# Sorted block attention with a two-layer network: instruction borders, order of loads and slots of work moved

## The chip, the cores and the metric

The kernel runs on one core of one Trainium2 chip. The metric is the device time of one execution in microseconds (us), as the median of several runs. A profile was taken of one execution; its times count from the start of its span. TensorE (PE in the profile, PEld for its weight loads) multiplies matrices, VectorE (DVE), ScalarE (ACT) and GpSimd (POOL) work on elements, SyncE (SP) issues transfers, and so does POOL here.

## The reference, cut to what matters

Four batches of eight heads, 768 tokens in eight blocks of 96, head size 64. A small 8x8 matrix for each head is normalized five times along its rows and columns (the Sinkhorn steps). It mixes the blocks of keys and values, and each block of queries attends to its mixed block. A two-layer network with a squared ReLU follows.

```python
P = sort_net                                  # (4, 8, 8, 8)
for _ in range(5):
    P = P - np.max(P, axis=-1, keepdims=True)
    P = np.exp(P)
    P = P / (np.sum(P, axis=-1, keepdims=True) + 1e-09)
    P = P / (np.sum(P, axis=-2, keepdims=True) + 1e-09)
k_sorted = np.einsum('bhij,bhjcd->bhicd', P, k_b)      # v_sorted likewise
scores = scale * np.matmul(q_b, k_sb.transpose(0, 1, 2, 4, 3))
attn = softmax(scores)
x = (attn @ v_sb)  # to (3072 tokens, 512)
h = x @ w_in                                  # 512 x 2048
g = s * np.maximum(h, 0) ** 2 + b
out = g @ w_out                               # 2048 x 512
```

Since out = s * (r*r) @ w_out + b * (column sums of w_out), the kernel adds b as a bias made of those column sums.

## The kernel before

The tokens are cut into eight tiles of 384, two for each batch. For each tile, `ffn1` is the first layer (64 products of 128x128 by 384 columns, eight pairs of PSUM banks) and `ffn2` the second (three blocks of 128 tokens, 16 products of 512 columns each). The attention of batch b+1 is laid between the products of batch b's second layer, by "slots": a table that names which piece is issued after which product. Batch 0's attention has nothing to hide behind, but its second half lies in the first layer of tile 0.

POOL issues the loads of k, q, v and of both weights, which come as float32 and land as bfloat16. PSUM has two pools here: `psa`, three buffers of two banks, and `psb`, two buffers of one bank.

The start, cut:

```python
    psa = ctx.enter_context(tc.tile_pool(name="psa", bufs=3, space=bass.MemoryType.PSUM))
    psb = ctx.enter_context(tc.tile_pool(name="psb", bufs=2, space=bass.MemoryType.PSUM))
# ...
    QTOK = {}

    def load_q(b):

        ti = rawp.tile([BLK, NB, H, D], BF, tag="rawq", name="qtok")
        qv = q[b].rearrange("h (n t) d -> t n h d", n=NB)
        for n in range(NB):
            nc.gpsimd.dma_start(out=ti[:, n], in_=qv[:, n])
        QTOK[b] = ti
# ...
    load("k", 0, 3)
    load_q(0)
    ones = const.tile([128, 32], BF)
    wi = const.tile([128, NHP, d_ff], BF)
    wo = const.tile([128, NF, d_model], BF)

    def load_w():
        wiv = moe_w_in.rearrange("(a p) f -> p a f", p=128)
        for c in range(2):
            cs = slice(c * (d_ff // 2), (c + 1) * (d_ff // 2))
            for a in range(NHP):
                nc.gpsimd.dma_start(out=wi[:, a, cs], in_=wiv[:, a, cs])
        fill_vs(0)
        wov = moe_w_out.rearrange("(f p) n -> p f n", p=128)
        for c in range(4):
            fs = slice(c * (NF // 4), (c + 1) * (NF // 4))
            nc.gpsimd.dma_start(out=wo[:, fs, :], in_=wov[:, fs, :])
# ...
    def warm(n, w=512):
        for _ in range(n):
            if not Z:
                Z.append(psb.tile([128, 512], FP, tag="b", name="z"))
            nc.tensor.matmul(out=Z[0][:, 0:w], lhsT=zeros[:, 0:128], rhs=zeros[:, 0:w],
                             start=True, stop=True)
# ...
    warm(60, 64)
    warm(30)
    for it in range(5):
        nc.scalar.activation(out=sn, in_=sn, func=AF.Exp)
        if it == 1:
            for d0 in range(0, D, D // 4):
                permute(nc.gpsimd, 0, v0f, slice(3 * CV, C2), slice(d0, d0 + D // 4))
        if 1 <= it <= 3:
            permute(nc.scalar, 0, v0f, slice((it - 1) * CV, it * CV))
        if it in (1, 2):
            idle[it - 1]()
        # ... sums, reciprocals and products of sn on DVE
```

`warm` keeps TensorE busy with products of zeros while DVE and ACT normalize `sn`. Each product of the kernel is two instructions, a weight load and a matmul. The normalized matrices are then spread over the partitions (`pe`), and turned into the moving matrices `pd` that mix keys and values:

```python
    def spread_p():

        PE_.append(psb.tile([128, B, NB, NB], FP, tag="b", name="pe"))
        for b in range(B):
            nc.tensor.matmul(out=PE_[0][:, b].rearrange("p i j -> p (i j)"), lhsT=emat[:, b, :],
                             rhs=sn.rearrange("p i j -> p (i j)"), start=True, stop=True)

    def take_p(b0, n):

        bs = slice(b0, b0 + n)
        tmp = rtp.tile([128, n * NB, NB], FP, tag=f"tmp{n}", name="tmp")
        nc.vector.tensor_tensor(out=tmp, in0=PE_[0][:, bs].rearrange("p b i j -> p (b i) j"),
                                in1=spread(jsel, [[0, n * NB], list(jsel.ap[1])]), op=ALU.mult)
        nc.vector.tensor_reduce(out=PT[:, bs].rearrange("p b i -> p (b i)"), in_=tmp, axis=AX.X,
                                op=ALU.add)
        cs = rtp.tile([128, n], FP, tag=f"cs{n}", name="cs")
        nc.vector.tensor_reduce(out=cs, in_=PT[:, bs], axis=AX.X, op=ALU.add)
        nc.vector.reciprocal(out=RC[:, bs], in_=cs)

    def build_pd(b):
        pd = const.tile([128, 2, 2, NG], BF, name=f"pd{b}")
        nc.vector.scalar_tensor_tensor(
            out=pd.rearrange("p e z (a i) -> p (e z a) i", i=NB),
            in0=spread(bm, [list(bm.ap[1]), [0, NB]]), scalar=RC[:, b:b + 1],
            in1=spread(PT[:, b], [[0, 4 * NHP], list(PT.ap[2])]), op0=ALU.mult, op1=ALU.mult)
        PD[b] = pd
```

Keys, values, scores, attention times values, and the transposes that make `xt` are pieces, of which `k_piece` shows the pattern; all but the transposes take a buffer of `psa`. Batches 1 to 3 have x transposed by a DMA (`t_dma`), and their queries likewise (`q_dma`).

```python
    def k_piece(b, c0, eng):
        src, mov, dst = RAW["k", b], PD[b], KS[b % 2]
        ps = psa.tile([128, CK, 2, NG], FP, tag="a", name="tp")
        for c in range(CK):
            for e in range(2):
                nc.tensor.matmul(out=ps[e * 64:(e + 1) * 64, c].rearrange("p z g -> p (z g)"),
                                 lhsT=src[:, c0 + c, :],
                                 rhs=mov[:, e].rearrange("p z g -> p (z g)"),
                                 start=True, stop=True)
        evac(eng, dst[:, :, :, c0:c0 + CK], ps.rearrange("p c z g -> p g z c"))
# ...
    def ffn1(t, slots, ahead=0):

        gt = gtp.tile([128, NF, TG], BF, tag="gt", name="gt")
        GT[t] = gt
        xt = XT.pop(t)
        H1 = {}

        def part(i, hpl):
            if i not in H1:
                H1[i] = psa.tile([128, 2, 512], FP, tag="a", name="hps")
            for f in range(2):
                for hp in hpl:
                    fc = (2 * i + f) * 128
                    nc.tensor.matmul(out=H1[i][:, f, 0:TG], lhsT=wi[:, hp, fc:fc + 128],
                                     rhs=xt[:, :, hp, :],
                                     start=(hp == 0), stop=(hp == NHP - 1))

        for i in range(ahead):
            part(i, (0, 1))
        for i in range(NF // 2):
            part(i, (2, 3) if i < ahead else range(NHP))
            rt = rtp.tile([128, 2, TG], BF, tag="rt", name="rt")
            h = H1.pop(i)[:, :, 0:TG]
            nc.scalar.activation(out=rt, in_=h, func=AF.Relu)
            nc.vector.tensor_tensor(out=gt[:, 2 * i:2 * i + 2, :], in0=rt, in1=rt, op=ALU.mult)
            for p in slots.get(i, ()):
                p()
```

`ffn2` runs its slots after every fourth product: slot m*4 + f//4. The order of the program after the Sinkhorn steps:

```python
    spread_p()
    take_p(0, 1)
    build_pd(0)
    warm(3)
    k_piece(0, 0, "A")
    k_piece(0, CK, "D")
    k_piece(0, 2 * CK, "A")

    nc.gpsimd.tensor_copy(out=ones[:, 0:1], in_=KS[0][:, 0, 0, 2 * CK:2 * CK + 1])
    load_w()
    q_piece(0, 0, "D")
    v_piece(0, 0, "A")
    v_piece(0, CK, "D")
    v_piece(0, 2 * CK, "A")
    v_piece(0, 3 * CK, "D")
    s_piece(0, 0, 0)
    s_piece(0, 0, 1)
    s_piece(0, 0, 2)
    warm(1)
    p_piece(0, 0, 0)
    s_piece(0, 0, 3)
    take_p(1, B - 1)
    warm(1)
    p_piece(0, 0, 1)
    warm(1)
    p_piece(0, 0, 2)
    Z.clear()
    t_piece(0, 0, 0, "A")
    p_piece(0, 0, 3)
    warm(3)
    t_piece(0, 0, 2, "D")
# ...
    def loads(b):
        load("k", b)
        load("v", b)
        load_q(b)
        v_sort(b)

    loads(1)
# ...
    def make_bias():
        cps = psa.tile([128, d_model], FP, tag="a", name="cps")
        for f in range(NF):
            r = slice(f % 4 * 32, f % 4 * 32 + 32)
            nc.tensor.matmul(out=cps[r], lhsT=ones, rhs=wo[:, f, :],
                             start=(f < 4), stop=(f >= NF - 4), tile_position=(0, f % 4 * 32))
        nc.vector.tensor_scalar(out=bias[0:32], in0=cps[0:32], scalar1=b_bc[0:32], scalar2=None,
                                op0=ALU.mult)
        for r in range(32, 128, 32):
            nc.vector.scalar_tensor_tensor(out=bias[0:32], in0=cps[r:r + 32], scalar=b_bc[r:r + 32],
                                           in1=bias[0:32], op0=ALU.mult, op1=ALU.add)
        for r in range(32, 128, 32):
            nc.scalar.copy(out=bias[r:r + 32], in_=bias[0:32])
# ...
    ffn1(0, {0: [QP(0, 1, "D")], 1: [SB(0, 1, 0)], 2: [SB(0, 1, 1)], 3: [P(0, 1, 0), SB(0, 1, 2)],
             4: [P(0, 1, 1), SB(0, 1, 3)], 5: [P(0, 1, 2)], 6: [P(0, 1, 3), TP(0, 1, 0, "A")],
             7: [TP(0, 1, 2, "D")]}, ahead=3)
    ffn1(1, {1: [PDB(1)], 3: [PDB(2)], 5: [PDB(3)], 6: [make_bias]}, ahead=3)
    for b in range(B):
        n = b + 1
        if b:
            if n < B:
                loads(n)
            ffn1(2 * b, {})
            ffn1(2 * b + 1, {})
        if n == B:
            ffn2(2 * b, {})
            ffn2(2 * b + 1, {})
            break
        q_dma(n)
        ffn2(2 * b, {0: [K(n, 0, "D"), K(n, 1, "A"), K(n, 2, "D")],
                     4: [V(n, 0, "D"), V(n, 1, "A"), V(n, 2, "D")],
                     8: [V(n, 3, "D"), SC(n, 0, 0), SC(n, 0, 1)],
                     11: [P(n, 0, 0), SC(n, 0, 2), SC(n, 0, 3)]})
        # ... the next tile's slots: the rest of the attention, t_dma after x
```

Of the kernel before, what the change touches and what calls it, by code (L numbers as in the profile page):

```python
# [22 lines left out]
def kernel(  # L23
# [66 lines left out]

    QTOK = {}

    def load_q(b):

        ti = rawp.tile([BLK, NB, H, D], BF, tag="rawq", name="qtok")
        qv = q[b].rearrange("h (n t) d -> t n h d", n=NB)
        for n in range(NB):
            nc.gpsimd.dma_start(out=ti[:, n], in_=qv[:, n])  # L98
        QTOK[b] = ti

    zeros = const.tile([128, 512], BF)
    nc.vector.memset(zeros, 0.0)  # L102
# [14 lines left out]
    nc.gpsimd.affine_select(out=emat, in_=emat, pattern=[[-H, B], [-1, H], [0, 2 * NB]], base=0,  # L117
                            channel_multiplier=1, compare_op=ALU.not_equal, fill=1.0)
    load("k", 0, 3)
    load_q(0)  # L120
    ones = const.tile([128, 32], BF)
    wi = const.tile([128, NHP, d_ff], BF)
    wo = const.tile([128, NF, d_model], BF)
# [1 line left out]
# [3 lines that stand above are left out]
            cs = slice(c * (d_ff // 2), (c + 1) * (d_ff // 2))  # L128
            for a in range(NHP):
                nc.gpsimd.dma_start(out=wi[:, a, cs], in_=wiv[:, a, cs])  # L130
        fill_vs(0)
        wov = moe_w_out.rearrange("(f p) n -> p f n", p=128)
        for c in range(4):
            fs = slice(c * (NF // 4), (c + 1) * (NF // 4))
            nc.gpsimd.dma_start(out=wo[:, fs, :], in_=wov[:, fs, :])
# [16 lines left out]
    def permute(eng, b, src, cs=slice(0, C2), ds=slice(0, D)):  # L152
# [4 lines left out]
        else:  # L157
# [14 lines left out]
    nc.vector.tensor_reduce(out=rstat, in_=sn, axis=AX.X, op=ALU.max)  # L172
    nc.vector.tensor_tensor(out=sn, in0=sn, in1=rstat.broadcast_to([BH, NB, NB]),
                            op=ALU.subtract)
    warm(60, 64)
    warm(30)
    for it in range(5):
        nc.scalar.activation(out=sn, in_=sn, func=AF.Exp)
        if it == 1:
            for d0 in range(0, D, D // 4):  # L180
                permute(nc.gpsimd, 0, v0f, slice(3 * CV, C2), slice(d0, d0 + D // 4))
        if 1 <= it <= 3:
            permute(nc.scalar, 0, v0f, slice((it - 1) * CV, it * CV))
        if it in (1, 2):
            idle[it - 1]()
        nc.vector.tensor_reduce(out=rstat, in_=sn, axis=AX.X, op=ALU.add)
        nc.vector.reciprocal(out=rrec, in_=rstat)
        nc.vector.tensor_tensor(out=sn, in0=sn, in1=rrec.broadcast_to([BH, NB, NB]), op=ALU.mult)
        if it == 4:
            break  # L190
        nc.vector.tensor_reduce(out=rstat, in_=sn.rearrange("p i j -> p j i"),
                                axis=AX.X, op=ALU.add)
        if it == 0:
            nc.vector.tensor_tensor(out=rstat, in0=rstat, in1=eps, op=ALU.add)
        nc.vector.reciprocal(out=rrec, in_=rstat)
        nc.vector.tensor_tensor(out=sn, in0=sn, in1=spread(rrec, [[0, NB], list(rrec.ap[1])]),
                                op=ALU.mult)
# [1 line left out]
    PD = {}  # L199
    PT = const.tile([128, B, NB], FP)  # L200
    RC = const.tile([128, B], FP)
    PE_ = []

    def spread_p():

        PE_.append(psb.tile([128, B, NB, NB], FP, tag="b", name="pe"))
        for b in range(B):
            nc.tensor.matmul(out=PE_[0][:, b].rearrange("p i j -> p (i j)"), lhsT=emat[:, b, :],
                             rhs=sn.rearrange("p i j -> p (i j)"), start=True, stop=True)

    def take_p(b0, n):

        bs = slice(b0, b0 + n)
        tmp = rtp.tile([128, n * NB, NB], FP, tag=f"tmp{n}", name="tmp")
        nc.vector.tensor_tensor(out=tmp, in0=PE_[0][:, bs].rearrange("p b i j -> p (b i) j"),
                                in1=spread(jsel, [[0, n * NB], list(jsel.ap[1])]), op=ALU.mult)
        nc.vector.tensor_reduce(out=PT[:, bs].rearrange("p b i -> p (b i)"), in_=tmp, axis=AX.X,
                                op=ALU.add)
# [5 lines that stand above are left out]
# [3 lines left out]
            in0=spread(bm, [list(bm.ap[1]), [0, NB]]), scalar=RC[:, b:b + 1],  # L227
            in1=spread(PT[:, b], [[0, 4 * NHP], list(PT.ap[2])]), op0=ALU.mult, op1=ALU.mult)
        PD[b] = pd

    def first_pd():
        spread_p()
        take_p(0, 1)
        build_pd(0)

    def evac(eng, out, in_):
        if eng == "A":
# [133 lines left out]
    def ffn1(t, slots, ahead=0):  # L371

        gt = gtp.tile([128, NF, TG], BF, tag="gt", name="gt")
        GT[t] = gt
        xt = XT.pop(t)
        H1 = {}

        def part(i, hpl):
# [8 lines that stand above are left out]

        for i in range(ahead):
            part(i, (0, 1))
        for i in range(NF // 2):  # L390
            part(i, (2, 3) if i < ahead else range(NHP))
            rt = rtp.tile([128, 2, TG], BF, tag="rt", name="rt")
# [5 lines that stand above are left out]
# [31 lines left out]
        nc.sync.dma_start(out=out[r0:r0 + 128, ns], in_=ot[:, ns])  # L429


    spread_p()
    take_p(0, 1)
    build_pd(0)
    warm(3)
    k_piece(0, 0, "A")
    k_piece(0, CK, "D")
# [12 lines left out]
    warm(1)  # L450
    p_piece(0, 0, 0)
    s_piece(0, 0, 3)
    take_p(1, B - 1)
    warm(1)
    p_piece(0, 0, 1)
    warm(1)
# [32 lines left out]
    def make_bias():  # L489
# [7 lines left out]
        for r in range(32, 128, 32):  # L497
            nc.vector.scalar_tensor_tensor(out=bias[0:32], in0=cps[r:r + 32], scalar=b_bc[r:r + 32],  # L498
                                           in1=bias[0:32], op0=ALU.mult, op1=ALU.add)
        for r in range(32, 128, 32):  # L500
            nc.scalar.copy(out=bias[r:r + 32], in_=bias[0:32])  # L501

# [8 lines left out]
    def QP(b, h, eng): return lambda: q_piece(b, h, eng)  # L511


    ffn1(0, {0: [QP(0, 1, "D")], 1: [SB(0, 1, 0)], 2: [SB(0, 1, 1)], 3: [P(0, 1, 0), SB(0, 1, 2)],
             4: [P(0, 1, 1), SB(0, 1, 3)], 5: [P(0, 1, 2)], 6: [P(0, 1, 3), TP(0, 1, 0, "A")],
             7: [TP(0, 1, 2, "D")]}, ahead=3)
    ffn1(1, {1: [PDB(1)], 3: [PDB(2)], 5: [PDB(3)], 6: [make_bias]}, ahead=3)
    for b in range(B):
        n = b + 1
        if b:  # L520
            if n < B:
                loads(n)
            ffn1(2 * b, {})
            ffn1(2 * b + 1, {})
        if n == B:
            ffn2(2 * b, {})
            ffn2(2 * b + 1, {})
            break
        q_dma(n)
        ffn2(2 * b, {0: [K(n, 0, "D"), K(n, 1, "A"), K(n, 2, "D")],  # L530
                     4: [V(n, 0, "D"), V(n, 1, "A"), V(n, 2, "D")],
                     8: [V(n, 3, "D"), SC(n, 0, 0), SC(n, 0, 1)],
                     11: [P(n, 0, 0), SC(n, 0, 2), SC(n, 0, 3)]})
        ffn2(2 * b + 1, {0: [P(n, 0, 1)], 1: [P(n, 0, 2)],
                         2: [P(n, 0, 3), TD(n, 0), SC(n, 1, 0), SC(n, 1, 1)],
                         4: [P(n, 1, 0)], 5: [P(n, 1, 1), SC(n, 1, 2), SC(n, 1, 3)],
# [31 lines left out]
```

The softmax here doesn't subtract the row's maximum and nothing guards it: scores larger than these inputs give would overflow.

## Time and profile before

The kernel takes 243.22 us (median of three runs, 243.13 to 243.81). The profiled execution has a span of 241.1 us.

| stage | from, us | to, us |
|---|---|---|
| warm-up of TensorE beside the Sinkhorn steps | 1.2 | 11.3 |
| `pe`, `pd`, keys, queries, values, scores of batch 0 | 11.3 | 29.6 |
| first layer of tiles 0 and 1 | 29.6 | 58.1 |
| column sums, bias, first keys of batch 1 | 55.6 | 65.5 |
| second layer of tiles 0 and 1, attention of batch 1 | 58.1 | 95.8 |
| first layer of tiles 2 and 3 | 95.8 | 116.8 |
| second layer of tiles 2 and 3, attention of batch 2 | 116.8 | 146.0 |
| the same for tiles 4 and 5 | 146.0 | 196.0 |
| tiles 6 and 7 | 196.0 | 241.1 |

| group | mean ns of one | count |
|---|---|---|
| hps, first layer, 384 columns | 326 | 512 |
| ops, second layer, 512 columns | 387 | 345 recorded |
| rt, ACT, 768 elements | 811 | 64 |
| gt, DVE, 768 elements | 597 | 64 |
| v moved by POOL (vp) | 884 | 24 |

Matmuls overlap, so a mean of 326 ns isn't what one adds: 128 of hps in a row take 20.80 us, 163 ns each. How to read the views: in the page, 40 slices show each engine's busy share in tenths, and PEclk the clock that TensorE was granted. A wait names the instruction that waited and what released it; "issue" means that the engine waited for nothing that the profile shows. The chain is the work that ended last, followed back from the end.

### The profile page before, as it was taken

Reading aid. Unit: us, or ns where it says so; the run is one execution under the profiler, and the core shown is the slowest. Engines: PE = TensorE matmul, PEld = TensorE weight load, DVE = VectorE, ACT = ScalarE, POOL = GpSimd, SP = SyncE. Lnnn points to the kernel's source line nnn. Section 1 sums busy time; section 2 is a strip of 40 time slices with the busy share of each in tenths; the row PEclk is TensorE's granted clock in tenths of the full one; section 3 lists DMA queues with packets and bytes.
Section 4 is the critical chain, followed back from the end, with each engine's and each line's share of the span. In section 5 each row is a group of like instructions: output and inputs, shape, how many; then the busy total and the mean of one; then the engine's idle time right before and its main releaser. Section 6 shows DMA issues by size and latency. Waiting matters only on the chain.

```text
span 241.1 us, 5694 instructions
## 1 busy us (share of the span) xinstructions
PE 221.9 (92%) x2481; PEld 133.0 (55%) x2507; DVE 122.6 (51%) x227; ACT 96.1 (40%) x124; POOL 65.3 (27%) x101
## 2 busy tenths in 40 slices
PE   7975979998499997999999999999999999999994
PEld 6464646664355653666655555666656556654453
DVE  6654735659536554434654763444656544442221
ACT  4635338562503350565512423565223416651000
POOL 8577742539919927400000000000000000000000
PEclk9998699999779999999999999999999999999999
DMA  6999999999799699990011189300111450001112
GB/s 199 207 121 143 204 206 199 205 133 141 131 184 170 110 200 178 189 154 0 3 46 46 54 145 174 69 0 0 49 43 46 109 155 0 0 4 45 60 71 87
DMA packets 52777, 25.80 MB, mean 107 GB/s; under 512 B 44816, under 2 KB 47120, under 8 KB 52752
## 3 DMA queue, kind: packets, MB, share of 16 engines
q0 software_dynamic: 29712, 12.85, 43.7%
q1 hardware_dynamic: 23040, 12.59, 22.8%
q8 instruction: 19, 0.31, 0.5%
q14 instruction: 6, 0.05, 0.1%
HBM read 27.27 MB, written 6.29 MB: 139 GB/s over the span
## 4 chain that ended last, share of the span: by engine, by line
PE 82%; DVE 6%; DMA 4%; issue 4%; ACT 3%
PE hps L384 32%; PE ops L405 30%; PE z L148 4%; DMA xt<-x 4%; PE tv L286 3%; PE pv L336 3%; PE sc L301 3%; PE tp L249 2%; ACT rt L394 2%; PE ops L418 1%; DVE gt L395 1%; DVE x L342 1%; DVE bias L498 1%; PE tq L268 1%; ACT bias L501 1%
## 5 line engine op out<-in xcount | busy, mean ns | idle before, releaser
L384 PE MATMUL hps<-xt,wi 128*128 128x384 bf16 x512 | 85.4, 326 | 1.7 <-DMA xt<-x 1.6
L405 PE MATMUL ops<-wo,gt 128*128 128x512 bf16 x345 | 83.5, 387 | 2.4 <-issue 1.6
L394 ACT ACTIVATE rt<-hps 128x768 bf16<-128x768 f32 x64 | 51.7, 811 | 53.2 <-PE hps L384 53.2
L384 PEld LDWEIGHTS <-wi 128*128 128x128 bf16 x512 | 49.3, 98 | 35.0 <-DMA xt<-x 2.1
L395 DVE TENSOR_TENSOR gt<-rt 128x768 bf16<-128x768 bf16 x64 | 38.2, 597 | 52.4 <-ACT rt L394 49.8
L405 PEld LDWEIGHTS <-gt 128*128 128x128 bf16 x368 | 34.3, 100 | 38.2 <-issue 3.0
L426 DVE SCALAR_TENSOR_TENSOR ot<-ops,s_bc,bias 128x512 f32<-128x512 f32 (+1 forms) x25 | 18.2, 730 | 41.1 <-PE ops L405 38.9
L306 ACT ACTIVATE at<-sc 112x768 bf16<-112x768 f32 x28 | 21.2, 807 | 34.3 <-PE sc L301 34.1
L98 POOL DMA_DIRECT2D qtok<-in_q_dram x32 | 24.7, 783 | 29.1 <-DMA rawk<-in_k_dram 10.4
L342 DVE TENSOR_TENSOR x<-pv,rec 96x512 bf16<-96x512 f32 x32 | 22.0, 687 | 1.1
L158 POOL COPY vp<-rawv 128x384 bf16<-128x384 bf16 x24 | 20.1, 884 | 0.0
L336 PEld LDWEIGHTS <-at 112*128 112x128 bf16 (+1 forms) x256 | 14.2, 106 | 7.0 <-issue 0.8
L240 DVE CAST vs<-tv 112x1024 bf16<-112x1024 f32 x11 | 13.2, 1222 | 5.6 <-PE tv L286 5.5
L336 PE MATMUL pv<-vs,at 112*128 112x66 bf16 (+1 forms) x256 | 14.8, 202 | 0.3 <-issue 0.3
L148 PE MATMUL z<-zeros 128*128 128x64 bf16 (+1 forms) x96 | 12.7, 301 | 1.6 <-DVE zeros L102 1.2
L238 ACT CAST vs<-tv 112x1024 bf16<-112x1024 f32 x5 | 5.1, 1018 | 17.1 <-PE tv L286 17.1
L249 PE MATMUL tp<-pd,rawk 128*64 128x64 bf16 x384 | 7.6, 200 | 4.4 <-ACT rt L394 2.0
L286 PEld LDWEIGHTS <-vp 128*64 128x64 bf16 x512 | 8.8, 113 | 3.6 <-issue 3.1
L286 PE MATMUL tv<-pd,vp 128*64 128x64 bf16 x512 | 9.8, 197 | 0.8 <-issue 0.7
L249 PEld LDWEIGHTS <-rawk 128*64 128x64 bf16 x384 | 7.0, 116 | 6.3 <-issue 6.3
L341 DVE RECIPROCAL rec<-pv 96x8 f32<-96x8 f32 x32 | 6.4, 199 | 7.9 <-PE pv L336 7.9
L301 PE MATMUL sc<-qt,ks 64*128 64x96 bf16 x224 | 7.9, 211 | 2.5 <-issue 2.5
(68 smaller groups left out, 100.6 us busy)
## 6 DMA issues: line engine op xcount, KB each, us to landing
out_dram<-ot SPq DMA_DIRECT2D x23, 256.0 KB, 2.5
qtok<-in_q_dram POOLq DMA_DIRECT2D x32, 96.0 KB, 10.9
rawk<-in_k_dram POOLq DMA_DIRECT2D x3, 768.0 KB, 7.7
rawv<-in_v_dram POOLq DMA_DIRECT2D x3, 768.0 KB, 12.0
wi<-in_moe_w_in_dram POOLq DMA_DIRECT2D x8, 256.0 KB, 8.5
wo<-in_moe_w_out_dram POOLq DMA_DIRECT2D x4, 512.0 KB, 13.6
v0f<-in_v_dram SPq DMA_DIRECT2D x4, 384.0 KB, 4.3
rawk<-in_k_dram POOLq DMA_DIRECT2D x3, 256.0 KB, 8.1
```

Of the source, the lines that this page charges most:

```text
L98: nc.gpsimd.dma_start(out=ti[:, n], in_=qv[:, n])
L148: nc.tensor.matmul(out=Z[0][:, 0:w], lhsT=zeros[:, 0:128], rhs=zeros[:, 0:w], start=True, stop=True)
L158: eng.tensor_copy(out=o, in_=i)
L249: nc.tensor.matmul(out=ps[e * 64:(e + 1) * 64, c].rearrange("p z g -> p (z g)"), lhsT=src[:, c0 + c, :], rhs=mov[:, e].rearrange("p z g -> ...
L286: nc.tensor.matmul(out=ps[z * GAP:(z + 1) * GAP, d, :], lhsT=VP[b % 2][:, d0 + d, :], rhs=PD[b][:, :, z, :], start=True, stop=True)
L306: nc.scalar.activation(out=at, in_=sc[0:KR, :, 0:TG], func=AF.Exp, scale=scale)
L336: nc.tensor.matmul(out=pv[0:m, e, n * VW:(n + 1) * VW], lhsT=atf[:, c0:c0 + m], rhs=VS[b % 2][:, e * NG + g0 + n, :], start=True, stop=True)
L342: nc.vector.tensor_tensor(out=x[:, :, hp * 128:(hp + 1) * 128].rearrange("p n (e d) -> p e n d", e=2), in0=pvv[:, :, :, 0:D], in1=rec.unsq ...
L384: nc.tensor.matmul(out=H1[i][:, f, 0:TG], lhsT=wi[:, hp, fc:fc + 128], rhs=xt[:, :, hp, :], start=(hp == 0), stop=(hp == NHP - 1))
L394: nc.scalar.activation(out=rt, in_=h, func=AF.Relu)
L395: nc.vector.tensor_tensor(out=gt[:, 2 * i:2 * i + 2, :], in0=rt, in1=rt, op=ALU.mult)
L405: nc.tensor.matmul(out=ops, lhsT=gt[:, f, m * 128:(m + 1) * 128], rhs=wo[:, f, :], start=(f == 0), stop=(f == NF - 1))
```

## The change

It has five parts. (1) The warm-up has 66 products more, small ones, so that the borders of the instruction blocks[...] fall elsewhere. (2) `pe` is made for batch 0 alone first; the others' part is copied from PSUM to SBUF by ACT, and used later, in the first layer of tile 1. (3) The last quarter of batch 0's v is moved by ACT and not by POOL, and the second half of q comes behind the first half of w_in, so that w_in can be issued once the keys are moved. (4) The slots of tile 0's first layer are shifted, the last transpose goes into tile 1, the column sums go to the end of tile 1's first layer, the bias's copies and the next batch's keys to later slots of the second layer. (5) The loads of batches 2 and 3 wait, by a one-element copy on POOL, for the first result of a first layer.

```diff
-    def load_q(b):
-        ti = rawp.tile([BLK, NB, H, D], BF, tag="rawq", name="qtok")
+    def load_q(b, ns=range(NB)):
+        if b not in QTOK:
+            QTOK[b] = rawp.tile([BLK, NB, H, D], BF, tag="rawq", name="qtok")
         qv = q[b].rearrange("h (n t) d -> t n h d", n=NB)
-        for n in range(NB):
-            nc.gpsimd.dma_start(out=ti[:, n], in_=qv[:, n])
-        QTOK[b] = ti
+        for n in ns:
+            nc.gpsimd.dma_start(out=QTOK[b][:, n], in_=qv[:, n])
# ...
     load("k", 0, 3)
-    load_q(0)
+    load_q(0, range(HB))
     ones = const.tile([128, 32], BF)
# ...
                 nc.gpsimd.dma_start(out=wi[:, a, cs], in_=wiv[:, a, cs])
+            if c == 0:
+                load_q(0, range(HB, NB))
         fill_vs(0)
# ...
                             op=ALU.subtract)
-    warm(60, 64)
-    warm(30)
+    warm(140, 64)
+    warm(16)
     for it in range(5):
         nc.scalar.activation(out=sn, in_=sn, func=AF.Exp)
-        if it == 1:
-            for d0 in range(0, D, D // 4):
-                permute(nc.gpsimd, 0, v0f, slice(3 * CV, C2), slice(d0, d0 + D // 4))
-        if 1 <= it <= 3:
+        if it >= 1:
             permute(nc.scalar, 0, v0f, slice((it - 1) * CV, it * CV))
# ...
     RC = const.tile([128, B], FP)
-    PE_ = []
-    def spread_p():
-        PE_.append(psb.tile([128, B, NB, NB], FP, tag="b", name="pe"))
-        for b in range(B):
-            nc.tensor.matmul(out=PE_[0][:, b].rearrange("p i j -> p (i j)"), lhsT=emat[:, b, :],
+    PB = const.tile([128, B - 1, NB, NB], FP)
+    def spread_p(b0, n):
+        pe = psa.tile([128, n, NB, NB], FP, tag="a", name="pe")
+        for b in range(n):
+            nc.tensor.matmul(out=pe[:, b].rearrange("p i j -> p (i j)"), lhsT=emat[:, b0 + b, :],
                              rhs=sn.rearrange("p i j -> p (i j)"), start=True, stop=True)
-    def take_p(b0, n):
+        return pe
+    def take_p(b0, n, pe):
# ...
         tmp = rtp.tile([128, n * NB, NB], FP, tag=f"tmp{n}", name="tmp")
-        nc.vector.tensor_tensor(out=tmp, in0=PE_[0][:, bs].rearrange("p b i j -> p (b i) j"),
+        nc.vector.tensor_tensor(out=tmp, in0=pe.rearrange("p b i j -> p (b i) j"),
                                 in1=spread(jsel, [[0, n * NB], list(jsel.ap[1])]), op=ALU.mult)
# ...
-    def first_pd():
-        spread_p()
-        take_p(0, 1)
-        build_pd(0)
# ...
         GT[t] = gt
-        xt = XT.pop(t)
+        xt = XT[t]
         H1 = {}
# ...
             part(i, (0, 1))
+        for p in slots.get(-1, ()):
+            p()
         for i in range(NF // 2):
# ...
-    spread_p()
-    take_p(0, 1)
+    take_p(0, 1, spread_p(0, 1))
     build_pd(0)
+    pe = spread_p(1, B - 1)
+    nc.scalar.copy(out=PB, in_=pe)
     warm(3)
# ...
     s_piece(0, 0, 3)
-    take_p(1, B - 1)
     warm(1)
# ...
+    def copy_bias():
         for r in range(32, 128, 32):
# ...
-    ffn1(0, {0: [QP(0, 1, "D")], 1: [SB(0, 1, 0)], 2: [SB(0, 1, 1)], 3: [P(0, 1, 0), SB(0, 1, 2)],
-             4: [P(0, 1, 1), SB(0, 1, 3)], 5: [P(0, 1, 2)], 6: [P(0, 1, 3), TP(0, 1, 0, "A")],
-             7: [TP(0, 1, 2, "D")]}, ahead=3)
-    ffn1(1, {1: [PDB(1)], 3: [PDB(2)], 5: [PDB(3)], 6: [make_bias]}, ahead=3)
+    ffn1(0, {2: [QP(0, 1, "D")], 3: [SB(0, 1, 0)], 4: [SB(0, 1, 1), P(0, 1, 0)],
+             5: [SB(0, 1, 2), P(0, 1, 1)], 6: [SB(0, 1, 3), P(0, 1, 2)],
+             7: [P(0, 1, 3), TP(0, 1, 0, "A")]}, ahead=3)
+    ffn1(1, {-1: [TP(0, 1, 2, "D")], 1: [lambda: take_p(1, B - 1, PB), PDB(1)], 4: [PDB(2)],
+             5: [PDB(3)], 7: [make_bias]}, ahead=3)
+    gate = const.tile([128, 1], BF)
+    def gated_loads(b):
+        def f():
+            nc.gpsimd.tensor_copy(out=gate, in_=GT[2 * b - 2][:, 0, 0:1])
+            loads(b)
+        return f
# ...
         if b:
-            if n < B:
-                loads(n)
-            ffn1(2 * b, {})
+            ffn1(2 * b, {0: [gated_loads(n)]} if n < B else {})
             ffn1(2 * b + 1, {})
# ...
         q_dma(n)
-        ffn2(2 * b, {0: [K(n, 0, "D"), K(n, 1, "A"), K(n, 2, "D")],
-                     4: [V(n, 0, "D"), V(n, 1, "A"), V(n, 2, "D")],
-                     8: [V(n, 3, "D"), SC(n, 0, 0), SC(n, 0, 1)],
-                     11: [P(n, 0, 0), SC(n, 0, 2), SC(n, 0, 3)]})
+        s0 = {1: [copy_bias]} if b == 0 else {}
+        s0.update({
+            2: [K(n, 0, "A"), K(n, 1, "D"), K(n, 2, "A")],
+            5: [V(n, 0, "D"), V(n, 1, "A"), V(n, 2, "D")],
+            9: [V(n, 3, "D"), SC(n, 0, 0), SC(n, 0, 1)],
+            11: [P(n, 0, 0), SC(n, 0, 2), SC(n, 0, 3)]})
+        ffn2(2 * b, s0)
         ffn2(2 * b + 1, {0: [P(n, 0, 1)], 1: [P(n, 0, 2)],
```

## The prediction

> **What bounds the kernel now.** I read the engine shares first, then the slices with the granted clock, then TensorE's waits, then the chain in order of time at the places where the slices dip, and last a table of stretches.
>
> ```profile
> PE 221.9 (92%) x2481; PEld 133.0 (55%) x2507; DVE 122.6 (51%) x227; ACT 96.1 (40%) x124; POOL 65.3 (27%) x101
> PE   7975979998499997999999999999999999999994
> PEclk9998699999779999999999999999999999999999
> q8 instruction: 19, 0.31, 0.5%
> ```
>
> TensorE is the bound: 92% busy and 82% of the chain. But part of that busy time is run at a reduced clock (the 8, 6 and 7, 7 of PEclk), and each reduction follows a dip of PE. TensorE's waits name what made the dips:
>
> ```profile
> PE sc L301 <- issue: 2.5, 1, 2.5
> PE tp L249 <- ACT rt L394: 2.0, 1, 2.0
> PE tp L249 <- DVE bias L498: 1.7, 1, 1.7
> PE hps L384 <- DMA xt<-x: 1.6, 1, 1.6
> PE tq L268 <- ACT rt L394: 0.9, 1, 0.9
> PE tv L286 <- issue: 0.7, 1, 0.7
> PE tp L249 <- DVE pd L225: 0.6, 1, 0.6
> ```
>
> The columns are total, count and longest. Nothing after 96 us is in this list beyond fractions; everything to be won lies ahead of that. The table of stretches (length, busy time and count of PE, PEld, DVE, ACT, POOL, then clock, DMA share, GB/s) shows [...]the size of the loss:
>
> ```profile
> 18.67:22.08 3.41, 1.49 (x60) 1.18 (x54) 2.27 (x2) 2.15 (x3) 3.26 (x9) 1.00 0.96 127
> 22.08:25.49 3.41, 2.38 (x35) 1.82 (x37) 0.89 (x3) 2.00 (x3) 1.84 (x3) 0.50 1.11 202
> 59.65:63.06 3.41, 0.69 (x32) 0.58 (x32) 1.54 (x3) 1.74 (x3) 3.41 (x6) 1.00 0.42 43
> 63.06:66.47 3.41, 2.09 (x35) 1.51 (x36) 2.41 (x3) 1.82 (x3) 3.12 (x5) 0.50 0.99 202
> 65.45:95.83 30.38, 28.27 (x343) 15.22 (x347) 16.46 (x27) 7.06 (x9) 18.78 (x25) 0.93 1.24 167
> 116.85:146.01 29.16, 28.52 (x442) 16.74 (x448) 17.19 (x28) 8.87 (x11) 0.00 (x0) 1.00 0.27 61
> ```
>
> The reader is to see two things. A stretch of 3.41 us in which PE is busy for 1.49 or 0.69 us is followed by half clock. And the second layer with the next batch's attention takes 29.16 us undisturbed (116.85 to 146.01), while the same work for the first batch takes from 58.10 to 95.83, 37.7 us: 8.6 us are lost there.
>
> [...] 4,988 records on PE over 19 packets are 262 each, and between the two "issue" waits at 16.68 and 20.28 us lie 118 tv and 10 sc products, each with its weight load: 256. [...] both waits fall in the loads' busy time. [...]
>
> **The change part by part.**
>
> *1. Borders.* 60 products of 64 columns plus 30 of 512 become 140 plus 16, so 66 more products, 132 more instructions: each later border moves 132 instructions (66 products) forward in the program. The old borders stood before the 11th tv and before the 11th sc. The new ones stand inside the tp products, near the 72nd tv, and inside the last pv of the first half. [...] Saved: 2.50 + 0.73 us, and the half clock from 22.08 us (24 pv products took 0.68 per 8 instead of the later 0.27, sc and tr likewise: about 1.5 us on the chain). I put 0.5 us against it for the third border. The warm-up's length: the 60 took 3.38 us, 56 ns each, which is cold. From about 5 us they should need some 34 ns (pv's 0.27 us per 8, 66 columns each). So 68 products cold until 5, 72 at 34 ns = 2.4, and 16 at 218 ns (6.53 us for 30) = 3.5: the end near 10.9 us, and sn is ready at 11.06 anyway.
>
> *2. pd.* Two of the eight pe products now precede the first take_p: 1.04 becomes 0.26 us, so 0.8 us off the chain to the first tp. The take_p of the other batches (0.34 + 0.36 + 0.19 + 0.18 = 1.1 us of DVE between x and rec) leaves the first half's chain for a place in the first layer of tile 1, where DVE has room. The price, a copy to SBUF by ACT, lies beside the warm-up. Saved: 0.7 + 1.1 = 1.8, of which I count 1.2, as PE had other work in part of it. Sum at the first hps: 3.2 + 1.5 + 1.2 - 0.5 = 5.4: at 24.3 instead of 29.6 us.
>
> *3. w_in.* The v permute leaves POOL for ACT's idle time and half of q moves behind the first half of w_in. In the kernel before, POOL's waits[...] show w_in landing piece by piece until about 31.8 us. Now POOL is free for it about 0.9 us earlier, but 0.39 MB of q[...] lie between its halves: the second half should land at 33 to 34 us. PE wants it in pair 4 of the first layer: 24.3 + 12 products and three half pairs (24 x 0.163 = 3.9) + tq 0.8 + one pair 1.3 + scb 0.3 = 30.6 us. So I expect a wait of about 3 us, and pair 4 starts at about 34 instead of 38.65 us: 4.7 of the 5.4 remain.
>
> *4. The slots of tile 0.* They move back by one or two, which hides tq's 0.9 us and scb's 0.4, but they crowd at the end: the first half of xt is now copied by ACT behind the last rt (0.8 us with PE waiting), and the second behind the first parts of tile 1 (0.6). Together about 1 us lost at the border of the tiles. The first layer of tile 1 then ends near 54 instead of 58.1 us.
>
> *5. The layer change.* The column sums (cps, 1.05 us of PE, paid before and after) move behind the last pair, the keys' products behind 12 ops products, the copies of bias behind that. The chain rt, gt, pd, gt, bias x4, copies x3, rt from 54.45 to 64.05 us then runs beside cps and 12 ops (1.05 + 2.55 us), and only the third keys' product needs the PSUM buffer that bias frees. Gained: the waits 2.0 + 1.7 + 0.6 with their small gaps, and the half clock from 63.06 to 69.9 us (15 ops took 5.59 instead of 3.2). Together 8.6 less the 1.6 of the next point: 7.0.
>
> *6. Gated loads.* Batch 2's and 3's loads now start in a first layer. In the kernel before, POOL ran ahead and they filled the DMA engines from 60 to 104 us, and the transposes of x took 9.9 to 10.6 us there against a median of 4.6. The 1.6 us wait at 94.2 us goes. A load of one batch took some 14 us of DMA (61 to 75 us) and the v moves 6.3 to 7.6 us: about 21, just what two first layers (2 x 10.4) give, and V comes 6.7 us into the second layer.
>
> The sum: 4.7 - 0.6 (point 4 net of what it hides) + 7.0 + 1.6 = 12.7. From it I take 1 us: POOL moves v of batch 1 only after the last q issue (52.15 us before, some 2.5 us later now, by the gap that w_in's later start leaves in the DMA), so six of its eight moves, 5.7 us, end at about 60.5, just when slot 5 asks for them. The gain is 11.7 us: 243.2 - 11.7 = 231.5 us.
>
> **The rivals.**
> *The loads bound the first 60 us.* What PE gains early it waits for at w_in's second half, q and batch 1's v. For it: DMA at 200 GB/s without a pause from 24 to 48 us. Against: the loads leave the DMA before 54 us, and the layer change's loss lies behind it. Then points 1 and 2 bring little: 234 to 236 us.
> *The new places make new starved windows.* A 3 us wait for w_in could [...]bring half clock: 2 to 3 us more. Against: 2.60 busy of 3.41 us (15.26 to 18.67) kept it[...]. 233 to 235 us.
> *The borders stall elsewhere.* [...] the third new border could wait 1 us, and the gated loads could meet borders later. But a block in the first layer lasts 128 x 0.163 = 21 us. About 232.5 us.
> *No rival wins:* w_in comes in time and all is gained: 228 us.
>
> **Range and chances.** Points 5 and 6 rest on measured idle time and full-clock durations: 8.6 us, nearly sure. Points 1 to 4 are between 0 and 6. So 227.5 to 236 us. Faster by over 2% means under 238.4; even half of the sum does that. Slower needs a new long stall: 2%.
>
> **What would show it.** Right: no "issue" wait over 0.5 us on tv or sc; PEclk without 6 and 7 after the warm-up; hps first near 24 us; a wait of hps for w_in in tile 0; ops without half clock after the layer change; xt's transposes near 4.6 us; the span from the second batch's first layer to the end still 145.3 us (95.83 to 241.1). Wrong: a window with half clock at 22 or 32 us, a wait of tv for POOL's moves over 1 us, or of qt for batch 2's late loads.

## The result: 1.5% faster, a third of the gain that was predicted

The changed kernel takes 239.64 us (239.17 to 240.33, four runs) against 243.51 us for the kernel before, measured beside it; the ratio is 0.985, with a 95% interval of 0.981 to 0.989. Predicted were 231.5 us and a range of 227.5 to 236. The span of the profiled execution went from 241.1 to 237.4 us.

The same three lines of the page of the changed kernel (engine shares, and the slices of PE and of its clock):

```profile
PE 220.0 (93%) x2573; PEld 132.2 (56%) x2573; DVE 131.4 (55%) x224; ACT 100.0 (42%) x129; POOL 64.3 (27%) x99
PE   7893399979979999999999999999999999999994
PEclk9998589999999999999999999999999999999999
```

Of the two dips of the clock the second is gone: at 63 to 70 us, where ops ran at half speed, it now stays whole. The first has become longer, 10.2 us of half clock (21.5 to 32 us) where the kernel before had 6.8 there, and the fourth and fifth slice of PE (18 to 30 us) are at 3. TensorE's waits (total, count, longest) say what it is. In the names, tp and tv are the products that mix keys and values, tq and tr the transposes of q and x, sc the scores (scb in the second half of batch 0), pv attention times values, cps the column sums:

```profile
PE pv L331 <- POOL vs L142: 7.2, 1, 7.2
PE tp L244 <- DVE bias L495: 1.4, 1, 1.4
PE z L150 <- DVE zeros L102: 1.2, 1, 1.2
PE hps L379 <- DVE rec L336: 1.0, 1, 1.0
PE pe L207 <- DVE sn L187: 0.9, 1, 0.9
PE hps L379 <- DVE xt L235: 0.6, 1, 0.6
```

Most waits of the list before are gone or small: no "issue" wait of 2.5 us on sc, no 2.0 for ACT, no 1.6 for xt; that of tp for bias is still 1.4 (1.7 before). In their place stands one that the kernel before did not have: the first pv waits 7.2 us for a fill by POOL. POOL's timeline (start, length, line, instruction, and in brackets its idle time before) shows how the fill came to be so late:

```profile
15.84 0.19 POOL L438 COPY ones<-ks 128x1 bf16<-128x1 bf16 x1 [8.28 <-ACT ks L233]
15.96 2.18 POOL L130 DMA_DIRECT2D wi<-in_moe_w_in_dram  x4
18.09 3.15 POOL L99 DMA_DIRECT2D qtok<-in_q_dram  x4
21.18 0.63 POOL L130 DMA_DIRECT2D wi<-in_moe_w_in_dram  x1
23.16 0.55 POOL L130 DMA_DIRECT2D wi<-in_moe_w_in_dram  x1 [1.35 <-DMA wi<-in_moe_w_in_dram]
24.84 0.53 POOL L130 DMA_DIRECT2D wi<-in_moe_w_in_dram  x1 [1.13 <-DMA wi<-in_moe_w_in_dram]
26.12 0.53 POOL L130 DMA_DIRECT2D wi<-in_moe_w_in_dram  x1 [0.75 <-DMA wi<-in_moe_w_in_dram]
26.64 0.23 POOL L140 MEMSET vs<- 112x128 bf16 x1
26.93 0.20 POOL L141 MEMSET vs<- 32x128 bf16 x1
27.19 0.20 POOL L142 MEMSET vs<- 16x128 bf16 x1
```

`fill_vs(0)` writes the columns of ones of `vs`, from which pv takes the softmax's sums. It is called inside `load_w`, behind the eight issues of w_in, and POOL's timelines have it there too. In the kernel before these eight went out without a wait, in 4.3 us, and the fills were done at 21.84 us, two us before pv (the last line is TensorE's):

```profile
16.82 4.29 POOL L130 DMA_DIRECT2D wi<-in_moe_w_in_dram  x8
21.03 0.29 POOL L138 MEMSET vs<- 112x128 bf16 x1
21.38 0.20 POOL L139 MEMSET vs<- 32x128 bf16 x1
21.64 0.20 POOL L140 MEMSET vs<- 16x128 bf16 x1
23.85 0.68 PE L336 MATMUL pv<-vs,at 112*128 112x66 bf16 x8 [0.33 <-issue]
```

Now four issues of q stand between them. They cost 3.15 us themselves, and from the tenth issue on POOL waits until an earlier w_in has landed. The fills end at 27.4 us, and pv starts at 27.44. Just before the first copy POOL was idle for 8.28 us, room enough for the fills.

The milestones of both kernels, and of the prediction, in us:

| | before | predicted | after |
|---|---|---|---|
| first hps of tile 0 | 29.6 | 24.3 | 32.7 |
| pair 4 of tile 0 | 38.7 | 34 | 39.5 |
| first layer of tile 1 ends | 58.1 | 54 | 60.2 |
| first hps of tile 2 | 95.8 | 84.1 | 92.0 |
| from there to the end | 145.3 | 145.3 | 145.4 |

(84.1 is 95.8 less the predicted 11.7. The third row holds the column sums, 1.05 us, before and in the prediction, which took 4.1 off the 58.1, but not after: they come behind it there.) The start lost 3.1 us where 5.3 were to be won. Between the end of the first layer and tile 2, 37.7 us became 31.8; without the column sums, which now lie in that stretch, it is 30.8, so the layer change and the gated loads won 7.0 of the 8.6 that points 5 and 6 of the prediction gave them. The rest of the kernel is as long as before.

### The profile page after: what moved, and what is told of

Read it like the earlier page. It is cut to its first block, busy times and chain, and to the rows that moved or that the text cites. A ratio compares the mean times of both kernels' runs of the same rounds, so it can differ in the third digit from the quotient of the medians.

```text
span 237.4 us, 5852 instructions
## 1 busy us (share of the span) xinstructions
PE 220.0 (93%) x2573; PEld 132.2 (56%) x2573; DVE 131.4 (55%) x224; ACT 100.0 (42%) x129; POOL 64.3 (27%) x99
## 3 DMA queue, kind: packets, MB, share of 16 engines
q1 hardware_dynamic: 23040, 12.59, 22.1%
## 4 chain that ended last, share of the span: by engine, by line
PE 80%; DVE 9%; DMA 4%; ACT 3%; POOL 1%; issue 1%
PE ops L402 33%; PE hps L379 31%; PE pv L331 4%; DMA wi<-in_moe_w_in_dram 3%; DVE gt L392 3%; PE tv L281 3%; PE sc L296 2%; PE tp L244 2%; ACT rt L391 2%; PE ops L415 1%; PE z L150 1%; DVE bias L495 1%; POOL wi L130 1%; ACT ks L233 1%; DMA sn<-in_sort_net_dram 1%
## 5 line engine op out<-in xcount | busy, mean ns | idle before, releaser
L402 PE MATMUL ops<-wo,gt 128*128 128x512 bf16 x368 | 85.7, 380 | 0.0
L391 ACT ACTIVATE rt<-hps 128x768 bf16<-128x768 f32 x64 | 51.0, 811 | 58.6 <-PE hps L379 47.5
L392 DVE TENSOR_TENSOR gt<-rt 128x768 bf16<-128x768 bf16 x64 | 50.4, 796 | 39.4 <-ACT rt L391 38.5
L402 PEld LDWEIGHTS <-gt 128*128 128x128 bf16 x368 | 33.6, 98 | 36.7 <-issue 0.4
L150 PEld LDWEIGHTS <-zeros 128*128 128x128 bf16 x165 | 7.9, 112 | 3.5 <-DVE zeros L102 1.2
L233 ACT CAST ks<-tp 128x1024 bf16<-128x1024 f32 x8 | 8.0, 1015 | 1.4 <-PE tp L244 1.4
L244 PE MATMUL tp<-pd,rawk 128*64 128x64 bf16 x384 | 7.1, 197 | 1.4 <-DVE bias L495 1.4
## 6 DMA issues: line engine op xcount, KB each, us to landing
rawv<-in_v_dram POOLq DMA_DIRECT2D x3, 768.0 KB, 10.4
```

The source lines that it names most:

```text
L402: nc.tensor.matmul(out=ops, lhsT=gt[:, f, m * 128:(m + 1) * 128], rhs=wo[:, f, :], start=(f == 0), stop=(f == NF - 1))
```

## The experiments

The kernel before, measured again beside these versions, had from 3 to 21 us of half clock from one execution to the next (mean clocks of 0.993 to 0.958) and took 238.3 to 250.4 us, the changed kernel 239.7 to 240.6; so the 1.5% above holds for its own executions only, the fastest of the kernel before are no slower than the changed kernel, and versions are compared above all with each other and by the milestones of their traces.

**1. The fills first.** The changed kernel, with the three fills moved into POOL's idle time ahead of w_in.

```diff
+    fill_vs(0)
     nc.gpsimd.tensor_copy(out=ones[:, 0:1], in_=KS[0][:, 0, 0, 2 * CK:2 * CK + 1])
     load_w()          # without fill_vs(0) inside
```

> The changed kernel with POOL's three fills of the ones columns of vs moved ahead of w_in's issues; nothing else differs. Theory (the 7.2 us wait of pv is POOL's program order: the fills stand behind eight w_in and four q issues[...]): pv no longer waits for POOL, no half clock at 24 to 32 us, first hps near 24.5 us instead of 32.7, then up to 3 us of waiting for w_in's second half at pair 4; 233 to 235 us. Rival (the loads bound the start, POOL's order only shows where it waits): the wait moves whole to w_in, pair 4 stays near 39 us, 238 to 240 us.

233.04 us (231.68 to 234.50); against the kernel before, fastest to fastest, 231.68 to 238.34. The fills now lie in POOL's idle time:

```profile
8.09 0.21 POOL L141 MEMSET vs<- 16x128 bf16 x1
16.07 0.19 POOL L438 COPY ones<-ks 128x1 bf16<-128x1 bf16 x1 [7.77 <-ACT ks L232]
```

The wait for POOL is gone, pv starts at 20.26 us, and the clock is whole in every slice. Some of TensorE's waits in this version:

```profile
PE hps L378 <- DMA wi<-in_moe_w_in_dram: 1.6, 2, 0.9
PE z L149 <- DVE zeros L102: 1.2, 1, 1.2
PE hps L378 <- DVE rec L335: 1.0, 1, 1.0
PE hps L378 <- DVE xt L234: 0.6, 1, 0.6
PE tq L262 <- DMA qtok<-in_q_dram: 0.3, 1, 0.3
```

The first hps comes at 25.05 us, pair 4 goes on at 34.34 after waits for w_in's second half, the first layer of tile 1 ends at 54.4, tile 2 starts at 85.1. Those are the predicted milestones (24.3, 34, 54, 84.1) within about a microsecond; at the third, with the column sums, it is 55.5 for 54. So what kept the changed kernel from them is the place of the fills in POOL's program, though single terms of the prediction are off too (points 1, 4 and 5 below). And the rival has a share: of the 7.6 us won at the first hps, 5.2 are left at pair 4, because w_in's second half is the next to bind.

**2. q's split alone.** The kernel before, with only q's second half moved between the halves of w_in.

```diff
-    load_q(0)
+    load_q(0, range(HB))
...
                 nc.gpsimd.dma_start(out=wi[:, a, cs], in_=wiv[:, a, cs])
+            if c == 0:
+                load_q(0, range(HB, NB))
```

> The kernel before with one part of the change alone: q's second half issued between the halves of w_in, ahead of the fills. Theory (four more issues ahead of the fills make POOL late): the fills end near 27 us instead of 21.8, pv waits for POOL until then instead of starting at 23.85, and the time is 3 to 5 us above the kernel before. Rival (the wait comes from POOL starting w_in earlier, or from the borders): within 1 us of the kernel before.

247.91 us (246.61 to 249.91) beside 246.47 for the kernel before: 1.4 us more by the medians, where 3 to 5 were expected, and the times alone decide little, as the kernel before spreads by 12 us. The two traces, at nearly the same mean clock (0.965 and 0.970), are 3.8 us apart, and all of it is there at tile 2 (99.6 against 95.8). POOL's timeline repeats the pattern, 1.6 us later:

```profile
27.71 0.53 POOL L130 DMA_DIRECT2D wi<-in_moe_w_in_dram  x1 [1.36 <-DMA wi<-in_moe_w_in_dram]
28.23 0.23 POOL L140 MEMSET vs<- 112x128 bf16 x1
28.51 0.20 POOL L141 MEMSET vs<- 32x128 bf16 x1
28.77 0.20 POOL L142 MEMSET vs<- 16x128 bf16 x1
```

pv waits 8.2 us for POOL. So neither the borders nor the earlier start of w_in made the wait: the four issues did.

**3. q whole again.** The changed kernel with q loaded at once ahead of w_in, the fills still behind w_in (the two lines of experiment 2 undone).

> The changed kernel with q loaded whole ahead of w_in again, the fills still behind w_in. Theory: with eight issues ahead of them the fills end near 21 us, so pv waits 1 to 2 us instead of 7.2, and w_in's second half comes without q in between; 232 to 235 us. Rival (q's place is of no weight): pv still waits about 7 us, 239 to 240 us.

233.32 us (231.92 to 234.55). The fills end at 21.1 us and pv waits 0.3, for issue. It ends where the fills first end, by another way: tv waits 1.3 us for issue at the border inside it (after the 72nd product) and the clock is at half for nearly all of 20 to 26 us (0.52 in that stretch), but w_in then comes without a wait, and pair 4 starts at 34.22 us. Why tv waits there isn't shown, and why both ways end at the same time stays open: here w_in's landing does not bind.

**4. The borders.** What a border is, the trace of the kernel before shows in part. The two waits for issue stand 128 products apart, and packets of the queue that the page calls "instruction" start at 15.06 and 20.40 us, 2.34 and 2.38 us before the waits end (17.40 and 22.78). That TensorE waited for these packets is inferred, as the profile names no engine for the queue, and when a packet was asked for isn't shown. First the longer warm-up alone on the kernel before, then, on the version with the fills first, the old warm-up back.

> The kernel before with the longer warm-up alone (140 small and 16 large products). Theory: the issue waits of 0.7 us on tv and 2.5 us on sc go, the next thing to release pv is POOL's fill at 21.8 us, so 2 us are gained, plus 1 to 2 us if the clock is not halved: 239.5 to 241.5 us. Rival (the borders wait as long elsewhere): 243 us, with an issue wait over 1 us on another piece.

244.52 us over twenty runs (238.43 to 247.84), beside 246.47 for the kernel before (238.34 to 250.42): the spread that the clock makes is larger than what was expected, so the time decides nothing. The trace says more: the issue waits on tv and sc are gone but for 0.3 us, yet pv then waits 1.15 us for the fill, which ends at 22.95, and starts at 23.00 instead of 23.85, and the first hps comes at 29.02 instead of 29.60. So behind the borders the fill stood next already. The borders were therefore tried the other way round:

```diff
-    warm(140, 64)
-    warm(16)
+    warm(60, 64)
+    warm(30)
```

> The version with the fills first, with the old warm-up (60 small and 30 large products), so the old borders. Theory[...]: sc waits 2 us or more for issue near 19 us, the clock is halved after it, part of it is hidden by the later wait for w_in's second half: 1 to 3 us slower than with the new borders (233.0), 234 to 236 us. Rival (the places of the borders do not matter once the fills are first): 232.5 to 233.5 us and no issue wait over 0.7 us.

233.48 us (232.66 to 233.87). The theory was right about the waits, and wrong about the time. TensorE's timeline of this version (weight loads left out):

```profile
15.92 0.35 PE L280 MATMUL tv<-pd,vp 128*64 128x64 bf16 x10
17.26 2.34 PE L280 MATMUL tv<-pd,vp 128*64 128x64 bf16 x118 [0.99 <-issue]
19.62 0.52 PE L295 MATMUL sc<-qt,ks 64*128 64x96 bf16 x10
22.92 0.74 PE L295 MATMUL sc<-qt,ks 64*128 64x96 bf16 x14 [2.78 <-issue]
```

The waits stand again before the 11th tv and the 11th sc, 128 products apart, so the borders are where the count put them, and the longer warm-up does move them. But although the first hps comes 3.9 us later (28.97 against 25.05), the first layer of tile 1 ends only 1.9 us later (56.3), and the time is that of the fills first (233.04 and, measured again, 233.69). What the new borders win is mostly waited for again at w_in: this version does not wait for it, and pair 4 starts at 35.78 against 34.34. The second trace of the fills first, at a mean clock of 0.993, spans 231.7 us, close to the 232.1 of this one (0.990); the first, at 1.000, spans 230.9.

**5. The gate of the later loads.** On the version with the fills first, batch 2's and 3's loads without their gate (`loads(n)` ahead of `ffn1(2 * b, ...)`, as before).

> The version with the fills first, with batch 2's and 3's loads no longer gated. Theory: x's transpose for tile 2 takes about 10 us instead of 4 to 5, hps waits 1.5 to 2.5 us for it: 234.5 to 235.5 us. Rival (the transposes have room anyway, as the second layer is now earlier): 233 us, no wait of hps for xt.

236.54 us (234.28 to 237.38), about 3 us more, but not by the expected way. The transposes of x landed in 4.6 and 11.9 us instead of 3.7 and 4.9, and yet hps did not wait for them. TensorE's waits after 60 us:

```profile
PE ops L401 <- issue: 1.9, 12, 0.2
PE hps L378 <- ACT rt L390: 1.9, 1, 1.9
PE tp L243 <- DVE bias L495: 0.2, 1, 0.2
```

ACT in turn waited for gt: one gt on DVE took 6.77 us, from 95.25, while POOL moved v in eight copies from 95.35 to 101.61. Ungated, the moves fall in the middle of a first layer, where PE needs the buffers that this gt holds up; gated, at its end, where PE goes on into the second layer. Of the 4.4 us between the two traces (235.3 and 230.9) this wait is 1.9. The other 2.6 were already there at tile 2 (87.7 against 85.1), with 6.8 us of half clock behind the wait for w_in; batch 2's loads were not yet issued then, so they aren't the gate's. The one run at full clock, 234.28, against 231.68 and 232.72 of the fills first at full clock, puts the gate at some 2 us.

**6. The layer change.** On the version with the fills first, the old slots of the column sums, the bias's copies, keys and values.

```diff
-             5: [PDB(3)], 7: [make_bias]}, ahead=3)     # and copy_bias in slot 1
+             5: [PDB(3)], 6: [make_bias]}, ahead=3)     # copies inside make_bias
-            2: [K...], 5: [V...], 9: [V...]
+            0: [K...], 4: [V...], 8: [V...]
```

> The version with the fills first, with the old places of the column sums, the bias's copies and the keys (slots 6, 0, 4, 8 in place of 7, 2, 5, 9). Theory: tp waits again 4 us in all for DVE and ACT, and ops run some 6.8 us at half clock: 6 to 8 us slower, 239 to 241 us. Rival (POOL's moves of v, which end at 62 us, bound the second layer's start whatever the layer change does): 2 us slower, 235 us.

239.51 us (238.66 to 240.13), 5.8 to 6.5 us above the fills first (233.69 and 233.04). TensorE's timeline:

```profile
57.91 0.69 PE L243 MATMUL tp<-pd,rawk 128*64 128x64 bf16 x32 [0.62 <-DVE bias L495]
60.65 0.69 PE L243 MATMUL tp<-pd,rawk 128*64 128x64 bf16 x32 [2.04 <-ACT rt L390]
61.60 4.99 PE L401 MATMUL ops<-wo,gt 128*128 128x512 bf16 x15 [0.26 <-issue]
66.53 1.71 PE L280 MATMUL tv<-pd,vp 128*64 128x64 bf16 x96
68.39 3.40 PE L401 MATMUL ops<-wo,gt 128*128 128x512 bf16 x15 [0.16 <-issue]
```

The two waits are back, and behind them 15 ops take 4.99 us, where the next 15 take 3.40: the clock is 0.76 in the stretch from 60 to 67 us and 1.00 from there to 74. Of the 7.0 us between the traces (237.9 and 230.9), 4.5 are there at tile 2 (89.6 against 85.1). Most of the rest comes at the two later layer changes, where tp waits 1.5 and 0.6 us for rt, which waits for a gt held up beside POOL's moves of v (6.99 us at the longest). The kernel before, with the same slots and no gate, has no such wait there, so this rest belongs to the old slots and the gate together. The layer change is the part of the change that carries it.

**7. The base again, and three ways to bring w_in earlier.** The changed kernel was run again beside the second half of experiment 4 and beside 5 and 6, and the fills first beside the three below.

> The changed kernel once more, as the base for the runs beside it: 239 to 240.5 us, pv waiting some 7 us for POOL's fill.

239.98 us, pv waiting 7.5 us.

> The version with the fills first once more, as the base for the runs beside it: 232 to 234 us, hps waiting 1 to 2 us for w_in at pair 4.

233.69 us (232.14 to 235.46), hps waiting 2.1 us for w_in.

The gate of w_in at the first move of keys (`in_=KS[0][:, 0, 0, 0:1]`):

> The version with the fills first, with w_in's issue gated to the first of the three moves of keys, not the last: 1 us earlier. Theory (w_in's second half is what bounds pair 4 now): the waits for q and w_in shrink from 1.9 us to below 1 us, 0.7 to 1 us faster than the version with the fills first. Rival[...]: tv waits over 1 us for issue, the clock is halved, no gain or up to 1 us slower.

232.52 us (231.15 to 233.48), 1.2 us faster than the fills first beside it. No wait for w_in or q; instead pv waits 1.3 us for issue, and inside pv lies the third border of the prediction's count. The theory is right about the waits for data, and the rival that TensorE then waits over 1 us for issue, though on pv and not on tv.

No gate at all:

> The version with the fills first, with no gate for w_in at all: issued from 8 us on. Theory[...]: tv waits 2 us or more for issue near 17 us, half clock after it, but no wait for w_in later; 233 to 235 us. Rival (the gate costs more than it saves): issue waits below 1 us, no wait for w_in, 230.5 to 231.5 us.

235.01 us (234.47 to 236.28), 1.3 us slower. As expected, tv waits over 2 us for issue:

```profile
15.73 1.43 PE L280 MATMUL tv<-pd,vp 128*64 128x64 bf16 x72
19.48 1.07 PE L280 MATMUL tv<-pd,vp 128*64 128x64 bf16 x56 [2.32 <-issue]
```

The wait stands after the 72nd tv, where the prediction put the new border. With w_in issued behind the keys' moves the wait there is 0.2 us (experiment 1).

The gate at the first move, and w_in in quarters of its columns, q's second half after the second:

```diff
-        for c in range(2):
-            cs = slice(c * (d_ff // 2), (c + 1) * (d_ff // 2))
+        for c in range(4):
+            cs = slice(c * (d_ff // 4), (c + 1) * (d_ff // 4))
...
-            if c == 0:
+            if c == 1:
                 load_q(0, range(HB, NB))
```

> The gate at the first move of keys, and w_in in quarters of its columns with q's second half after the second quarter. Theory: pair 4 needs only the third quarter, which lands some 2 us before the whole second half: no wait for w_in, 1 to 2 us faster than the version with the fills first, near 231.5 us. Rival (POOL's sixteen issues at 0.55 us[...] hold the loads back): w_in waits stay, no gain.

230.46 us (229.53 to 230.78), 3.2 us faster than the fills first beside it and 9.2 below the changed kernel's 239.64. hps no longer waits for w_in, no issue wait is above 0.4 us, the clock is whole, and tile 2 starts at 83.2 us. This version beats both kernels. But two things changed in it. With the earlier gate alone hps does not wait for w_in either, so what the quarters add, 2.1 us by the medians, isn't the expected landing of the third quarter: in the traces the first hps comes at 24.50 instead of 25.79 us, as pv's issue wait of 1.3 us is down to 0.2. Why the finer division spares that wait isn't shown.

## Why the prediction was wrong, point by point

*1. Borders: the waits right, their worth wrong.* In the changed kernel no issue wait on PE is above 0.2 us (2.5 and 0.7 before). But the 4.7 us put on them (3.2 of waits and 1.5 of half clock) were hidden behind pv's wait here, and in experiment 4 the new borders' lead of 3.9 us at the first hps is down to 1.4 at pair 4, since w_in binds there: the medians do not tell old and new borders apart. The prediction's own numbers say so: it let w_in hold pair 4 at 34 us and PE want it at 30.6, so without the 4.2 us of the borders pair 4 would come at 34.8. Its 0.5 us for the third border was an estimate; experiment 1 shows 0.46 there. The 1.5 was also misread: 0.68 us for 8 pv is from the first start to the last end, and read so they take 0.43 at full clock; 0.27 is what they add to the chain. From pv to the first hps the changed kernel takes 5.26 us at half clock, experiment 1 takes 4.79 at full clock with those 0.46: some 0.9 us. The warm-up's small products, which the prediction calls cold until 5 us, have records of 242 ns up to 4.3 us in the changed kernel's trace and of 193 from 4.5 on, at a granted clock of 1.00 throughout; the warm-up ended at 10.4 us (predicted 10.9).

*2. pd: right.* The first tp starts at 13.02 instead of 13.76 us, 0.74 for the predicted 0.8.

*3. w_in: here the prediction failed.* It said that "POOL is free for it about 0.9 us earlier" and counted what q's bytes cost the DMA engines. It did not count what q's issues cost POOL, nor ask what stands behind them in POOL's program: the fills of `vs`, which pv waits for. It even used POOL's waits for w_in (2.3 us in three, ahead of wo's issues), but only to date its landing. The missed term is 7.2 us of PE time, and what shows it was in the profile before: the fills were done two us ahead of pv, and four issues of 0.78 us are longer than that, without any wait for an earlier load. The expected 3 us wait for w_in did not show, as pv's longer wait hid it; with the fills first it is 1.6 to 2.1 us.

*4. The slots of tile 0: right but for scb.* The list of waits has the two at the border of the tiles, 1.0 and 0.6 us (predicted 0.8 and 0.6), and tq's 0.9 is gone. scb's wait, which was to be hidden, is still 0.5 (0.4 before).

*5. The layer change: right in mechanism, a size off.* The half clock and the chain of 10 us went from PE's path, but tp still waits 1.4 us for bias, most of what is missing from the 8.6. In the changed kernel take_p and the pd's run on DVE beside POOL's moves of v; gt takes 3.45 us for 3 there, and DVE begins bias at 63.38, 2.1 us after cps is done. In experiment 1, where the first layer ends (54.4) before the moves begin (55.3), the same wait is 0.3.

*6. Gated loads: right in the changed kernel.* The transposes landed in 3.8 and 5.0 us, and the wait for xt is gone. Experiment 5 adds that on a faster base the gate is worth about as much for another reason.

The sum of the points, 231.5, was missed by 8.1 us; moving the fills gives back 6.0 to 6.9 (from 239.64 and 239.98 to 233.69 and 233.04).

The rival "the loads bound the first 60 us" gave 234 to 236, and "new starved windows" 233 to 235. Both saw a loss at the right place for the wrong reason: the stretch without work for PE (busy for 0.29 us from 20 to 26) came from POOL's order. Half clock followed from 21.5 us on, the PEclk slice of 5. Of the signs named beforehand, the issue waits, ops at full clock, the transposes and the last 145 us came out right; the first hps near 24 us, the whole clock after the warm-up and a wait of hps for w_in did not, and "a window with half clock at 22 or 32 us", a sign of being wrong, came (21.5 to 32).

## What to carry to other kernels

When issues are added to an engine's program, read what stands behind them in that program, and who waits for it: a load is paid for at its issuer too (0.53 to 0.78 us each here), and where the issuer has to wait for an earlier load to land (0.75 to 1.35 us before each of three issues here), everything behind it waits too. Small fills that need no data belong into an idle stretch ahead of the loads (6.0 to 6.9 us here). And a gain ahead of a transfer's landing is only worth what is left when that transfer binds; here an earlier issue of the transfer in finer pieces was worth 3.2 us, and the borders nothing that the medians show.

## What had not been expected of the hardware

One gt on DVE was held up through a whole series of copies on POOL. The spread of gt on DVE in the kernel before and in the changed one, and of the latter's copies on POOL (count: shortest/median/longest ns):

```profile
L395 DVE TENSOR_TENSOR gt<-rt x64: 551/559/1319, 33.2 to 217.7; 128x768 bf16<-128x768 bf16 x64
L392 DVE TENSOR_TENSOR gt<-rt x64: 544/559/6881, 36.3 to 214.0; 128x768 bf16<-128x768 bf16 x64
L160 POOL COPY vp<-rawv x24: 809/839/1192, 53.2 to 162.5; 128x384 bf16<-128x384 bf16 x24
```

A gt of 0.56 us took 6.88: from 107.36 us, 0.17 ahead of a series of eight copies, to 114.24, 0.4 after its end. In experiment 1 one began 0.66 us ahead of the first copy, while POOL issued its last load of q, and took 7.35. Both ended 0.4 us after the eighth copy. In both kernels no gt is held up so long beside batch 1's copies: the longest gt of the kernel before took 1.32 us, of the changed kernel beside those copies 1.26. What holds gt up, and what makes the difference, isn't settled by these runs.

Half clock came in steps here. In the traces it lasted twice 6.8 us (the kernel before, 22.1 to 28.9 and 63.0 to 69.9), 10.2 (the changed kernel) and 6.8 (experiment 5), and by their mean clocks some 3.2 (experiment 1 again, 0.993) and 17.1 us in all (experiment 2, 0.965): close to multiples of 3.41 us, the stretch of the table in the prediction. The mean clock of an execution mostly lies on 0.993, 0.986 and so on, in steps of 0.007 (3.4 us at half clock in a span of 240): 52 of the 57 executions of the kernel before that were measured beside the versions do. One to six such steps went with times from 238.3 to 250.4 us of that kernel; the version with quarters kept to 229.5 to 230.8 at 0.998 or more.
